# The low parts of `g` and of the expert weights, subtracted on VectorE instead of GpSimd

## The chip, the core and the metric

The kernel runs on one core of one Trainium2 chip. The metric is the device time of one execution in microseconds, as the median of several runs. The engines of a core are TensorE (PE: matrix products; PEld is its weight load), VectorE (DVE), ScalarE (ACT), GpSimd (POOL) and SyncE (SP, which here only issues DMAs). Each engine works through its own instructions in order and waits on semaphores for the others.

## What is computed

Three stages follow one another on 1792 tokens of 768 features:

```python
# 1. causal attention, 4 batches x 12 heads x 448 tokens x 64
scores = scale * np.matmul(q, k.transpose(0, 1, 3, 2))
scores = np.where(mask, -1000000000.0, scores)
x = softmax(scores) @ v                      # laid out as 1792 x 768
# 2. expansion with elu, 768 -> 2048 -> 768
h = x @ w_in
g = np.where(h > 0.0, h, alpha * (np.exp(np.minimum(h, 0.0)) - 1.0))
x = g @ w_out
# 3. routing to 8 experts of 224 tokens, in falling order of the logits
logits = x @ w_gate
order = np.argsort(-logits.flatten())        # greedy: one expert a token, at most 224 tokens an expert
for e in range(E):
    out[mask_e] = np.maximum(x[mask_e] @ w1[e], 0.0) @ w2[e]
```

## The kernel before, in words

**Products in two parts.** Where float32 accuracy is needed, an operand is split into a high part, which ScalarE copies into the format float32r, and a low part, the operand minus its high part. A product is then three products of TensorE: high by high, high by low, low by high. This gives the pairs of names `wh`, `wl` (weights), `xh`, `xl`, `gh`, `gl`. The change is about which engine subtracts the low parts.

**Stages.** Attention of the four batches runs interleaved with the first expansion (`gemm1`, L365), which writes `g` to DRAM as `gT_d`. Then comes the second expansion (`gemm2`, L592): 14 chunks of 128 tokens, for each 16 steps `m` of six products (L629). Every half chunk it loads a tile `gr` of 128x1024 (`load_g`), copies it to `gh` on ScalarE (L581) and subtracts `gl` (L582), which makes 28 of them. Beside it, interleaved into TensorE's order, runs the routing (`route`, L720): 7 phases, each with 7 search rounds. A round is a chain between VectorE and TensorE: `gg` (comparison, L757), products `lg` (L762), `fl` (L764), product `pv` (L767), `ju` (L770), next `gg`. A phase ends with `NB` (L798), products (L803, L806), `dd` (L809), a dozen small VectorE operations and the first `gg` of the next phase. Last come the 8 experts (`ffn`, L909). An expert's first half has 8 blocks of 6 pairs of products into a PSUM tile `h` (L928, L925; two buffers), each followed by `t` on ScalarE (L935), `t` on VectorE (L938), `ht` high on ScalarE (L941) and `ht` low on VectorE (L944). Its second half has 8 blocks of 12 products (L980), and TensorE's transposes of the next expert's tokens lie among them (L901). At its end the result `y` is copied (L956, L957) and scattered to `out` by an indirect DMA of GpSimd (L959); the next expert's tokens `xg` are gathered by two more (L889).

**Weights.** Each expert has 16 chunks of 128x768. `load_ck` loads one into one of 16 buffers `wr` through the sync engine's queue, 14 chunks ahead; `split_ck` copies it to `wh` on ScalarE (L504) and subtracts `wl` (L505), 7 chunks ahead of its use. Of 128 such chunks the even ones were subtracted on VectorE and the odd ones on GpSimd.

**Order.** The program is written by a small scheduler (`Sched`). Generators yield the estimated time of their products, and `after(d, fn)` puts a dependent operation behind them by `d` nanoseconds of that time. In the routing a negative yield says how much time of products of the second expansion lies before the next link of the chain:

```python
yield -1400 if n < 64 else -2200      # L759, between gg and lg
```

The operation then stands at that place in its engine's order, so that a subtraction placed between two links of the routing is executed between them.

Of the kernel before, what the change touches and what calls it, by code (L numbers as in the profile page):

```python
# [8 lines left out]
F32 = mybir.dt.float32  # L9
# [14 lines left out]
DM = H * D  # L24
KT = DM // 128
DF = 2048
MT = DF // 128
# [3 lines left out]
CAP = NTOK // E  # L31
# [3 lines left out]


class Sched:
    """Program order: products follow one another, and what depends on them is put behind
    them by about the time after which it can run."""

    def __init__(self):
        self.now, self.heap, self.n = 0.0, [], 0
# [1 line left out]
    def after(self, d, fn):  # L44
        self.n += 1
        tok = [False]
        heapq.heappush(self.heap, (self.now + d, self.n, fn, tok))
        return tok
# [28 lines left out]
def body(ctx, tc, q, k, v, w_in, w_out, w_gate, w1, w2, out, dbg=None):  # L77
    nc = tc.nc
    sch = Sched()
    after, need = sch.after, sch.need  # L80
    PE, V, A, G, SP = nc.tensor, nc.vector, nc.scalar, nc.gpsimd, nc.sync
# [5 lines left out]

    gT_d = dram.tile([128, MT, NTOK], F32, name="gT_d")

    # ---- constants  # L90
    ident = const.tile([128, 128], F32, name="ident")
    jp = const.tile([128, 128], F32, name="jp")
    mask = const.tile([128, S], F32, name="mask")
# [2 lines left out]
    wp = const.tile([128, MT, 32], F32, name="wp")  # L96
# [26 lines left out]
    for i in range(3):  # L123
        t = at.tile([128, NQ, 2, 64], F32, name=f"qz{i}", bufs=1)
        qz.append(t)

    # ---- loads
    KN, VN, WIN, STG = {}, {}, {}, {}

    def load_qk(n):  # L130
# [9 lines left out]
        SP.dma_start(VN[n][:, 0:3], v[b, j, 0:384].rearrange("(t p) h d -> p t h d", p=128))  # L140
        SP.dma_start(VN[n][:64, 3], v[b, j, 384:])

    # ---- float64 words to float32: bytes 3..6 hold the low exponent bits and the mantissa,
    # byte 7 the sign and the high exponent bits
    def load64_in(m):
        st = wf.tile([128, DM * 8], U8, name="st")
        STG[m] = st
        SP.dma_start(st[:, :DM * 8 - 3], w_in[m].bitcast(U8)[:, 3:])
# [38 lines left out]
        if nxt < MT:  # L187
            after(3100, lambda: load64_in(nxt))

    # ---- attention  # L190
    ST, XH, XL = {}, {}, {}

    def front(n):
# [91 lines left out]
            except StopIteration:  # L285
                st.remove(s)

    # ---- gate weights folded through w_out: wp = w_out @ w_gate, in stages of one chunk each
    def fold():
        ct, wt, wpt = {}, {}, {}  # L290

# [48 lines left out]

    WP = {}

    # ---- first expansion: gT = elu(w_in^T x)
    def logit4(pl, m, gs):
        for c in range(4):
            PE.matmul(pl[32 * c:32 * c + 32, :S], wp[:, m + c], gs[c],
# [71 lines left out]
    def logits(b, pl, tag):  # L418
        LT = wk.tile([128, S], F32, name="e")
        after(300, lambda: V.tensor_copy(LT, pl[:, :S]))  # L420

        # tokens on partitions
        def turn_logits():
            p = ps.tile([128, NQ, E], F32, name=tag, bufs=1)
            h, u = b * NQ, 0
            while u < NQ:
                n = 1 if (h + u) % 2 or u == NQ - 1 else 2
                o = 64 * ((h + u) % 2)
                PE.matmul(p[o:o + 64 * n, (h + u) // 2 - h // 2], LT[:, 64 * u:64 * (u + n)], sel, start=True, stop=True,
                          skip_group_check=True)  # L430
                u += n
            c0, c1 = (h + 1) // 2, (h + NQ) // 2
            V.tensor_copy(L[:, c0:c1], p[:, c0 - h // 2:c1 - h // 2])
            if h % 2:
                V.tensor_copy(L[64:, h // 2], p[64:, 0])
            else:
                V.tensor_copy(L[:64, c1], p[:64, c1 - h // 2])

        L_TOK.append(after(1500, turn_logits))
# [39 lines left out]
    def seq(*gs):  # L479
        for g in gs:  # L480
            yield from g

    sch.drive((seq(*[att_l(n) for n in range(-1, 6)]), 54000))
    for b in range(3):
        g = [(seq(*[att_l(n) for n in range(6 * b + 6, 6 * b + 12)]), 45000), (gemm1(b), 57600)]
# [11 lines left out]
    stAA.close()  # L497
    wA = ctx.enter_context(tc.tile_pool(name="wA", bufs=9, side="right"))

    # ---- weights of the later products: split into two parts that float32r carries  # L500
    def split(raw, pool, shape, e, gap=800):
        wh = pool.tile(shape, F32R, name="wh")
        wl = pool.tile(shape, F32R, name="wl")
        A.copy(wh, raw)  # L504
        return wh, wl, after(gap, lambda: e.tensor_sub(wl, raw, wh.bitcast(F32)))  # L505

    WO, WR = {}, {}
# [10 lines left out]
                yield -200  # L518
            WO[m] = split(WR.pop(m), wA, [128, DM], V)

    # logits of the first batch, from its part of gT
    def logits0():
        pl = ps.tile([128, 512], F32, name="pv", bufs=1)
        G0 = {}
# [15 lines left out]

    g0 = stA.enter_context(tc.tile_pool(name="g0", bufs=3))

    # ---- second expansion: x2 = g w_out
    # a row of zeros lies before the last chunk
    LAST = NTOK - 128
    x2_d = dram.tile([NTOK + 1, DM], F32, name="x2_d")
    stB, stW = ExitStack(), ExitStack()
    gb = stB.enter_context(tc.tile_pool(name="gb", bufs=3, side="right"))
    GR, GS = {}, {}

    # ---- weights of the experts: chunks of 128 rows of hidden features
    NCK = 2 * FT
    CK = {}

# [10 lines left out]

    def split_ck(i):
        if i < E * NCK:
            CK[i] = split(WR.pop(MT + i), wA, [128, DM], (V, G)[i % 2])
            load_ck(i + 14)

    def load_g(i):
# [5 lines left out]
    def split_g(i):  # L577
        t = GR.pop(i)
        gh = gb.tile([128, 8, 128], F32R, name="gh")
        gl = gb.tile([128, 8, 128], F32R, name="gl")  # L580
        A.copy(gh, t)  # L581
        GS[i] = gh, gl, after(1200, lambda: G.tensor_sub(gl, t, gh.bitcast(F32)))  # L582

    RT = []

# [59 lines left out]
        for _ in fg:  # L645
            yield 0

    # ---- the first expert's tokens: rows of the last chunk come from its product itself, by a
    # one-hot product, the others by a gather in which a row of zeros stands for those of the last chunk
    X2, PX, SLOT = {}, [], {}  # L650
    FIRST = {4: 1, 12: 1, 13: 1, 14: 1}

    def first_rows():
# [23 lines left out]
        for c in range(KT):  # L677
            PE.matmul(PX[c // 2][:, c % 2], o[:, c * 128:(c + 1) * 128], oh, start=False, stop=True,
                      skip_group_check=True)

    # ---- routing: the pairs in falling order of their logits, up to CAP tokens for an expert
    # keys of two parts: the upper 24 bits, then the lower 8 with the place of the token
    ROUNDS = (((18, 63), (12, 63), (6, 63), (0, 63)), ((12, 2 * NTOK // 32 - 1), (6, 63), (0, 63)))

    def consts_route(rt):
# [34 lines left out]
    def route():  # L720
# [55 lines left out]
        for ph in range(E - 1):  # L776
            V.tensor_tensor(lm, L, bc(pen, E), op=OP.add)
            V.tensor_reduce(m, lm, axis=AX.X, op=OP.max)
            # the bits of a float in an order of integers, in two halves
            V.tensor_scalar(mi, m.bitcast(I32), 31, -2 ** 31, op0=OP.arith_shift_right, op1=OP.bitwise_or)  # L780
            V.tensor_tensor(lm, lm, be(m, E), op=OP.is_equal)
            V.tensor_tensor(mi, mi, m.bitcast(I32), op=OP.bitwise_xor)
            V.tensor_tensor(lm, lm, bc(C["wt"], E), op=OP.mult)
            V.tensor_single_scalar(kh, mi, 8, op=OP.logical_shift_right)
            V.tensor_reduce(key, lm, axis=AX.X, op=OP.max)
            V.tensor_single_scalar(kl, mi, 0xFF, op=OP.bitwise_and)
            V.tensor_tensor(lm, lm, be(key, E), op=OP.is_equal)
            V.tensor_tensor(B, lm, be(un, E), op=OP.mult)
            V.scalar_tensor_tensor(m, kl, float(NTOK), C["rid"], op0=OP.mult, op1=OP.add)
            yield -1500 if ph else -9000  # L790
            th = yield from search(kh, 0.0, 0)
            V.scalar_tensor_tensor(key, kh, th, m, op0=OP.is_equal, op1=OP.mult)
            V.tensor_scalar(k2, kh, th, float(2 ** 20), op0=OP.is_gt, op1=OP.mult)
            V.tensor_add(key, key, k2)
            yield -500
            th = yield from search(key, 1.0, 1)
            V.tensor_scalar(k2, key, th, None, op0=OP.is_ge)
            V.tensor_tensor(NB_, B, be(k2, E), op=OP.mult)  # L798
            V.scalar_tensor_tensor(un, key, th, un, op0=OP.is_lt, op1=OP.mult)
            V.tensor_add(asg, asg, NB_)  # L800
            yield -400
            p = ps.tile([128, 512], F32, name="pv", bufs=1)
            PE.matmul(p[:, :NT * E], ones, NB_.rearrange("p c e -> p (c e)"), start=True, stop=True)  # L803
            p2 = ps.tile([128, 512], F32, name="lg", bufs=1)
            for c in range(NT):
                PE.matmul(p2[:E, :1], NB_[:, c], ones[:, :1], start=(c == 0), stop=(c == NT - 1))  # L806
            yield 400
            # a full expert takes no more part: its room is set beyond every count
            V.tensor_reduce(dd, p[:, :NT * E].rearrange("p (c e) -> p e c", e=E), axis=AX.X, op=OP.add)  # L809
            V.tensor_sub(rec[:E, 0:1], rec[:E, 0:1], p2[:E, :1])  # L810
            V.tensor_sub(rem, rem, dd)
            V.tensor_scalar(rec[:E, 1:2], rec[:E, 0:1], 0.5, 1.0e6, op0=OP.is_lt, op1=OP.mult)
            V.tensor_scalar(pen, rem, 0.5, -3.0e38, op0=OP.is_lt, op1=OP.mult)
            V.tensor_add(rec[:E, 0:1], rec[:E, 0:1], rec[:E, 1:2])
            yield -300
# [2 lines left out]
        V.tensor_add(asg, asg, B)  # L818
        V.memset(B, 0.0)
        yield -400  # L820
        # places within the experts, then the token of each place
        p = ps.tile([128, 512], F32, name="lg", bufs=1)
        PE.matmul(p[:, :NT * E], C["up"], asg.rearrange("p c e -> p (c e)"), start=True, stop=False,
                  skip_group_check=True)
# [53 lines left out]
    ex = ctx.enter_context(tc.tile_pool(name="ex", bufs=2))  # L878
    ix = IDX[0]

    # ---- experts
    XG = {}
    scat = []

# [24 lines left out]
    def ffn(e):  # L909
# [5 lines left out]
        for m in range(FT):  # L915
# [16 lines left out]
            t = ex.tile([128, 2, CAP], F32, name="t")  # L932
# [32 lines left out]
            after(300 + 400 * j, ev)  # L965

        W2 = {}
        # the last expert's halves follow one another, so that the first is written while the second is computed
        order = [(m, j) for j in range(2) for m in range(FT)] if e == E - 1 else \
            [(m, j) for m in range(FT) for j in range(2)]  # L970
        for m, j in order:
# [67 lines left out]
```

## Time and profile before

| | |
|---|---|
| median of 3 runs | 1116.58 us (1112.84 to 1119.04) |
| profiled execution: span from first to last instruction, the only time the page gives of it | 1113.1 us |
| PE busy | 1057.9 us, 95% |
| PEld busy | 881.7 us, 79% |
| DVE busy | 671.4 us, 60% |
| ACT busy | 438.9 us, 39% |
| POOL busy | 430.9 us, 39% |
| second expansion with routing | about 490 to 812 us of the span |
| experts | about 812 to 1106 us of the span |

Busy time is the time in which an engine has an instruction on record, and that holds time in which the instruction itself is held up. A wait is put down to what released it last. An `x2` behind a row of a timeline means two instructions in a row, merged. [...]

### The profile page before, as it was taken

The numbers are of one execution on the slowest core, as the hardware profiler recorded it, in microseconds if no ns is written. First come the engines' busy times: TensorE is split into PE (matmuls) and PEld (weight loads), VectorE is DVE, ScalarE is ACT, GpSimd is POOL, SyncE is SP. The second block draws the span as 40 slices with busy tenths as digits, with TensorE's granted clock in tenths as the row PEclk, the third lists the DMA queues.
The fourth block names the chain that finished last, engine by engine and source line by source line (L and its number), as shares of the span: only waits on it lengthen the run. The fifth ranks groups of instructions, "written<-read, shape, count | busy, mean of one in ns | idle before, by whom it ended". The sixth has DMA issues, their size and how long they took to land.

```text
span 1113.1 us, 17985 instructions
## 1 busy us (share of the span) xinstructions
PE 1057.9 (95%) x6615; PEld 881.7 (79%) x6615; DVE 671.4 (60%) x1596; ACT 438.9 (39%) x960; POOL 430.9 (39%) x467
## 2 busy tenths in 40 slices
PE   8999998999999999999999999989999999999997
PEld 4568676676777777878888888878988988898887
DVE  5889876777545445556545544553665466556652
ACT  5654444444445443432010001100255555455541
POOL 4465653444444440013222211322335455545542
PEclk9999999999999999999999999999999999999999
DMA  7646545666312106653233321220456676665710
GB/s 174 165 122 210 192 132 180 201 208 203 115 59 83 42 35 229 196 177 100 81 110 100 115 81 52 70 87 15 137 185 211 192 226 209 211 192 184 237 37 25
DMA packets 110858, 155.33 MB, mean 140 GB/s; under 512 B 29617, under 2 KB 82353, under 8 KB 110770
## 3 DMA queue, kind: packets, MB, share of 16 engines
q1 hardware_dynamic: 108210, 143.17, 40.8%
q0 software_dynamic: 2560, 11.01, 3.3%
q8 instruction: 52, 0.85, 0.3%
q14 instruction: 36, 0.29, 0.1%
HBM read 122.17 MB, written 31.98 MB: 138 GB/s over the span
## 4 chain that ended last, share of the span: by engine, by line
PE 77%; DVE 12%; issue 4%; ACT 4%; DMA 2%; SPq 0%; POOLq 0%; ACTq 0%; DVEq 0%; POOL 0%
PE h L629 11%; PE tp L629 9%; PE h L377 7%; PE sc L980 6%; PE h L379 6%; PE h L378 6%; PE h L928 5%; PE sc L200 5%; PE pv L262 4%; PE pv L980 3%; PE lg L980 3%; PE tp L248 3%; PE h L925 3%; PE lg L762 2%; DVE gg L757 2%
## 5 line engine op out<-in xcount | busy, mean ns | idle before, releaser
L582 POOL TENSOR_TENSOR gl<-gr,gh 128x1024 fp32r<-128x1024 f32 x28 | 72.2, 2595 | 305.1 <-ACT gh L581 195.6
L377 PE MATMUL h<-xh,wh 128*128 128x448 f32 x384 | 174.1, 453 | 0.0
L505 POOL TENSOR_TENSOR wl<-wr,wh 128x768 fp32r<-128x768 f32 x64 | 120.8, 1894 | 97.9 <-ACT wh L504 66.9
L928 PE MATMUL h<-xt,wh 128*128 128x448 f32 x384 | 130.1, 396 | 17.8 <-DVE t L938 17.8
L227 POOL TENSOR_SCALAR s<-s,sm 128x448 f32<-128x448 f32 (+6 forms) x168 | 98.4, 597 | 109.0 <-DVE sm L220 76.2
L379 PE MATMUL h<-xh,wl 128*128 128x448 f32 x384 | 140.5, 366 | 0.0
L378 PE MATMUL h<-xl,wh 128*128 128x448 f32 x384 | 140.2, 365 | 0.0
L212 ACT ACTIVATE s<-s,sm 128x448 f32<-128x448 f32 (+6 forms) x168 | 85.1, 507 | 136.5 <-DVE sm L208 135.1
L362 POOL TENSOR_TENSOR wl<-wr,wh 128x768 fp32r<-128x768 f32 x48 | 92.0, 1918 | 103.7 <-ACT wh L361 97.6
L504 ACT CAST wh<-wr 128x768 fp32r<-128x768 f32 x144 | 118.2, 829 | 31.3 <-PE lg L980 19.1
L639 ACT COPY x<-h 128x384 f32<-128x384 f32 x14 | 6.7, 480 | 261.5 <-PE h L629 261.5
L505 DVE TENSOR_TENSOR wl<-wr,wh 128x768 fp32r<-128x768 f32 x80 | 90.8, 1139 | 30.1 <-ACT wh L504 29.6
L377 PEld LDWEIGHTS h<-xh,wh 128*128 128x128 f32 x384 | 72.4, 189 | 37.3 <-issue 28.8
L208 DVE CUSTOM_DVE_ANT_0 s<-sc,mask 128x448 f32<-128x448 f32 (+6 forms) x150 | 62.1, 420 | 61.8 <-PE sc L200 56.2
L925 PE MATMUL h<-xt,wl 128*128 128x224 f32 x384 | 96.3, 278 | 0.0
L200 PE MATMUL sc<-kT,qz 128*128 128x192 f32 (+6 forms) x300 | 92.1, 395 | 1.9 <-DMA kT<-in_k_dram 1.0
L928 PEld LDWEIGHTS h<-xt,wh 128*128 128x128 f32 x384 | 73.6, 202 | 24.8 <-DVE t L938 20.1
L629 PE MATMUL h<-wh,gh 128*128 128x384 f32 x224 | 87.3, 390 | 0.0
L378 PEld LDWEIGHTS h<-xl,wh 128*128 128x128 f32 x384 | 72.8, 190 | 8.7 <-issue 3.0
L925 PEld LDWEIGHTS h<-xt,wl 128*128 128x128 f32 x384 | 78.0, 203 | 2.0
L379 PEld LDWEIGHTS h<-xh,wl 128*128 128x128 f32 x384 | 72.2, 188 | 6.1
L629 PE MATMUL h<-wl,gh 128*128 128x384 f32 x224 | 76.1, 340 | 0.3 <-DVE wl L505 0.3
(206 smaller groups left out, 2292.7 us busy)
## 6 DMA issues: line engine op xcount, KB each, us to landing
wr<-in_moe_w_dram SPq DMA_DIRECT2D x128, 384.0 KB, 3.6
gT_d<-g SPq DMA_DIRECT2D x64, 224.0 KB, 1.9
gr<-gT_d SPq DMA_DIRECT2D x28, 512.0 KB, 4.2
st<-in_moe_w_in_dram SPq DMA_DIRECT2D x16, 767.6 KB, 4.5
st<-in_moe_w_out_dram SPq DMA_DIRECT2D x16, 767.6 KB, 5.0
wo_d<-wo SPq DMA_DIRECT2D x16, 384.0 KB, 3.0
wr<-wo_d SPq DMA_DIRECT2D x16, 384.0 KB, 3.8
qz<-in_q_dram SPq DMA_DIRECT2D x48, 112.0 KB, 3.6
```

Of the source, the lines that this page charges most:

```text
L200: PE.matmul(p[:, :w], qT[:, i].rearrange("p a c -> p (a c)"), kT[:, :w], start=True, stop=True)
L227: G.tensor_scalar(s[:, :w], s[:, :w], sm[:, 2, i:i + 1], 1.0, op0=OP.mult, op1=OP.mult)
L362: t = after(800, lambda: (V if b == 3 else G).tensor_sub(wl, WIN[m], wh.bitcast(F32)))
L377: PE.matmul(p[:, :S], wh[:, c], xh, start=(c == 0), stop=False)
L378: PE.matmul(p[:, :S], wh[:, c], xl, start=False, stop=False)
L379: PE.matmul(p[:, :S], wl[:, c], xh, start=False, stop=(c == KT - 1))
L504: A.copy(wh, raw)
L505: return wh, wl, after(gap, lambda: e.tensor_sub(wl, raw, wh.bitcast(F32)))
L629: PE.matmul(p[n][:, :384], st[:, mm], wsel[:, 384 * n:384 * n + 384], start=(m == 0 and first), stop=(m == MT - 1 and st is gl))
L925: PE.matmul(p[:, :CAP], wl[:, c], xt[:, c, :CAP], start=False, stop=stop, skip_group_check=True)
L928: PE.matmul(p[:, :2 * CAP], wh[:, c], xt[:, c], start=(c == 0), stop=(c == KT - 1), skip_group_check=True)
L980: PE.matmul(acc[j][n][:HC, :384], ht[:, m, s, j * HC:(j + 1) * HC], wsel[:, 384 * n:384 * n + 384], start=(m == 0 and first), stop=(m == F ...
```

## The change

In `split_ck` all weight chunks of the experts now give their subtraction to VectorE (`V`) instead of to VectorE and GpSimd (`G`) in turn, and in `split_g` the subtraction of `gl` is VectorE's. Nothing else is changed but comments, which are left out here.

```diff
     def split_ck(i):
         if i < E * NCK:
-            CK[i] = split(WR.pop(MT + i), wA, [128, DM], (V, G)[i % 2])
+            CK[i] = split(WR.pop(MT + i), wA, [128, DM], V)
             load_ck(i + 14)
...
     def split_g(i):
         t = GR.pop(i)
         gh = gb.tile([128, 8, 128], F32R, name="gh")
         gl = gb.tile([128, 8, 128], F32R, name="gl")
         A.copy(gh, t)
-        GS[i] = gh, gl, after(1200, lambda: G.tensor_sub(gl, t, gh.bitcast(F32)))
+        GS[i] = gh, gl, after(1200, lambda: V.tensor_sub(gl, t, gh.bitcast(F32)))
```

TensorE's 6016 and ScalarE's 731 rows of the program are the same and stand in the same order. On VectorE 28 rows of `gl` and 64 of `wl` are added. Three places show it.

VectorE at the end of an expert's first half, before (the last blocks of the first expert, `t`, `wl` and `ht`, and the first `wl` of its second half):

```order
L938 TENSOR_TENSOR t_8556<-h_8538,t_8556 128x224
L505 TENSOR_TENSOR wl_8558<-wr_8198,wh_8557 128x768
L944 SCALAR_TENSOR_TENSOR ht_8392<-t_8556,ht_8392 128x224
L938 TENSOR_TENSOR t_8580<-h_8562,t_8580 128x224
L944 SCALAR_TENSOR_TENSOR ht_8392<-t_8580,ht_8392 128x224
L505 TENSOR_TENSOR wl_8608<-wr_8254,wh_8607 128x768
```

The same place now:

```order
L938 TENSOR_TENSOR t_8556<-h_8538,t_8556 128x224
L505 TENSOR_TENSOR wl_8558<-wr_8198,wh_8557 128x768
L944 SCALAR_TENSOR_TENSOR ht_8392<-t_8556,ht_8392 128x224
L938 TENSOR_TENSOR t_8580<-h_8562,t_8580 128x224
L505 TENSOR_TENSOR wl_8586<-wr_8233,wh_8585 128x768
L944 SCALAR_TENSOR_TENSOR ht_8392<-t_8580,ht_8392 128x224
```

A `wl` stands between `t` and `ht` in every block, where it stood in every second one.

GpSimd between two experts, before (`xg` the gathers, `out_dram` the scatters, `spacer` a memset of one element):

```order
L889 DMA xg<-x_d,ig 112x768 x2
L958 MEMSET spacer 1x1
L959 DMA out_dram<-y,ix 1792x768
L505 TENSOR_TENSOR wl<-wr,wh 128x768 x8
L958 MEMSET spacer 1x1
L959 DMA out_dram<-y,ix 1792x768
```

The same place now:

```order
L889 DMA xg<-x_d,ig 112x768 x2
L958 MEMSET spacer 1x1
L959 DMA out_dram<-y,ix 1792x768
L958 MEMSET spacer 1x1
L959 DMA out_dram<-y,ix 1792x768
```

The eight subtractions are gone, and DMA issues and memsets of one element are what remains in GpSimd's order.

VectorE in the routing, the difference at two places, a search round and the end of a phase:

```order
 L754 MEMSET base_5347 128x1
 L757 SCALAR_TENSOR_TENSOR gg_5348<-key_5352,base_5347,tab12_5310 128x14x111
+L582 TENSOR_TENSOR gl_6048<-gr_5817,gh_6047 128x1024
 L764 TENSOR_SCALAR fl_5350<-lg_6056,rec_5336 8x111
 L770 TENSOR_SCALAR ju_5351,base_5347<-pv_6079,base_5347 128x111
...
 L799 SCALAR_TENSOR_TENSOR un_5330<-key_5352,base_5347,un_5330 128x14
 L800 TENSOR_TENSOR asg_5332<-asg_5332,NB_5346 128x112
+L582 TENSOR_TENSOR gl_6169<-gr_5929,gh_6168 128x1024
 L809 TENSOR_REDUCE dd_5349<-pv_6181 128x8
 L810 TENSOR_TENSOR rec_5336<-rec_5336,lg_6183 8x1
```

Of the 28 `gl`, 20 now stand between a `gg` and its `fl`, as in the first piece. The other eight: two among the last operations of the first expansion, one ahead of the first phase's search, one ahead of a phase's second search, one ahead of `dd` (second piece), one ahead of a phase's first `gg`, one ahead of the operations that make `NB`, and one behind the last phase.

## Rows read from the trace of the kernel before

**Rows 1.** Page, busy us, share of the span, instructions.
```profile
PE 1057.9 (95%) x6615; PEld 881.7 (79%) x6615; DVE 671.4 (60%) x1596; ACT 438.9 (39%) x960; POOL 430.9 (39%) x467
```

**Rows 2.** Waits of TensorE from 485 us on: us in total, times, longest.
```profile
PE h L928 <- DVE t L938: 17.8, 8, 2.3
PE lg L762 <- DVE gg L757: 10.9, 8, 3.8
PE pv L803 <- DVE NB L798: 2.4, 1, 2.4
```

**Rows 3.** Timeline of VectorE in the seventh expert: start us, us, instruction, idle before.
```profile
1039.64 4.49 DVE L944 SCALAR_TENSOR_TENSOR ht<-t,ht 128x224 fp32r<-128x224 f32 x1 [0.46 <-ACT ht L941]
1044.05 0.38 DVE L938 TENSOR_TENSOR t<-h,t 128x224 f32<-128x224 f32 x1
1044.35 0.94 DVE L505 TENSOR_TENSOR wl<-wr,wh 128x768 fp32r<-128x768 f32 x1
1045.22 0.38 DVE L944 SCALAR_TENSOR_TENSOR ht<-t,ht 128x224 fp32r<-128x224 f32 x1
1045.85 0.39 DVE L938 TENSOR_TENSOR t<-h,t 128x224 f32<-128x224 f32 x1 [0.25 <-ACT t L935]
```

**Rows 4.** Timeline of GpSimd, same stretch.
```profile
1039.28 0.96 POOL L959 DMA_INDIRECT out_dram<-y,ix  x1 [0.22 <-issue]
1040.26 3.61 POOL L505 TENSOR_TENSOR wl<-wr,wh 128x768 fp32r<-128x768 f32 x2
```

**Rows 5.** Timeline of TensorE, same stretch.
```profile
1044.48 0.47 PE L928 MATMUL h<-xt,wh 128*128 128x448 f32 x1 [2.33 <-DVE t L938]
```

**Rows 6.** Timeline of VectorE in the second expansion.
```profile
525.24 1.14 DVE L757 SCALAR_TENSOR_TENSOR gg<-kh,base,tab 128x882 bf16<-128x882 int32 x1
527.70 0.27 DVE L764 TENSOR_SCALAR fl<-lg,rec 8x63 bf16<-8x63 f32 x1 [1.31 <-PE lg L762]
...
550.28 1.14 DVE L757 SCALAR_TENSOR_TENSOR gg<-kh,base,tab 128x882 bf16<-128x882 int32 x1
...
742.61 2.19 DVE L811 TENSOR_TENSOR rem<-rem,dd 128x8 f32<-128x8 f32 x1
```

**Rows 7.** Timeline of GpSimd at the last of these.
```profile
742.38 4.74 POOL L582 TENSOR_TENSOR gl<-gr,gh 128x1024 fp32r<-128x1024 f32 x2 [17.34 <-ACT gh L581]
```

**Rows 8.** Busy times by expert: stretch, length, PE, PEld, DVE, ACT, POOL, PEclk, DMA, GB/s.
```profile
849.30:886.60 37.30, 34.99 (x205) 33.46 (x205) 21.26 (x29) 19.88 (x38) 19.23 (x14) 0.95 0.66 207
886.60:922.40 35.80, 33.46 (x206) 32.12 (x205) 21.97 (x29) 19.66 (x38) 19.32 (x14) 1.00 0.68 215
```

**Rows 9.** Busy times of two stretches of the second expansion, columns as in rows 8.
```profile
550.00:600.00 50.00, 47.56 (x357) 41.71 (x356) 24.15 (x67) 5.51 (x8) 9.40 (x4) 0.97 0.29 90
...
750.00:812.00 62.00, 60.50 (x442) 55.70 (x442) 30.33 (x69) 11.42 (x17) 16.09 (x8) 0.97 0.23 75
```

**Rows 10.** Instructions by tile and line: count, ns min/median/max, first and last start.
```profile
L505 DVE TENSOR_TENSOR wl<-wr,wh x80: 940/948/6394, 439.1 to 1088.6; 128x768 fp32r<-128x768 f32 x80
...
L269 DVE TENSOR_TENSOR xl<-pv,xh x24: 602/624/625, 19.2 to 422.2; 128x448 fp32r<-128x448 f32 x24
...
L582 POOL TENSOR_TENSOR gl<-gr,gh x28: 2337/2398/3442, 490.7 to 791.1; 128x1024 fp32r<-128x1024 f32 x28
```

**Rows 11.** The last expert's first half on TensorE, columns as in rows 10.
```profile
L928 PE MATMUL h<-xt,wh x48: 362/375/473, 1071.7 to 1089.0; 128*128 128x448 f32 x48
```

**Rows 12.** Timeline of TensorE at the second phase's first `gg`.
```profile
551.76 0.57 PE L762 MATMUL lg<-gg,B 128*8 128x63 bf16 x14
```

**Rows 13.** Timeline of GpSimd in the first expert.
```profile
815.56 0.93 POOL L889 DMA_INDIRECT xg<-x_d,ig  x1 [11.57 <-DMA x_d<-x]
```

**Rows 14.** Timeline of VectorE in the first expert.
```profile
815.58 0.96 DVE L505 TENSOR_TENSOR wl<-wr,wh 128x768 fp32r<-128x768 f32 x1
```

## The prediction

> **What bounds the kernel now.** I read the page's busy shares first, then the list of who waited for whom on TensorE, then the timelines of single engines at the stalls, and last the busy times cut at the eight experts. TensorE is busy 95% of the span, VectorE 60% [rows 1]. So work that moves from GpSimd to VectorE has no price by itself. It counts only where TensorE waits for VectorE, or would begin to.
>
> After the first expansion TensorE has three waits worth counting, and all are for VectorE [rows 2]: 17.8 us in 8 waits for `t` (L938) in the experts, 10.9 us in 8 waits for `gg` (L757) and 2.4 us in one wait for `NB` (L798), both in the routing that runs beside the second expansion. The reader is to see that the other lines of that list, left out here, stay under 0.6 us each.
>
> What holds VectorE? Each expert shows the same picture near its start. `ht` (L944), an operation of 0.38 us, is on record with 4.49 us: the fourth row against the first of [rows 3]. GpSimd runs a DMA issue and then two weight subtractions (L505) back to back from 1040.26 for 3.61 us [rows 4], so to 1043.87, and the next `t` starts at 1044.05. TensorE, which has two PSUM buffers `h` and needs one of them back, goes on at 1044.48 after 2.33 us of waiting [rows 5]. So an elementwise operation on GpSimd and a VectorE operation with two SBUF inputs exclude one another, and GpSimd's next one goes ahead of the waiting VectorE. Routing shows it as well: `rem` (L811), on 8 columns, is on record with 2.19 us from 742.61, while GpSimd runs two `gl` subtractions (L582) from 742.38 for 4.74 us [rows 6, 7].
>
> A stall is dearer than its wait. The expert from 886.6 has its wait too, but keeps a granted clock of 1.00 and takes 35.80 us; its neighbour reads 0.95 and takes 37.30 [rows 8]. [...] One such drop costs 37.3 - 35.8 = 1.5 us. In the second expansion two stretches read 0.97 [rows 9]; the two longest waits there, 2.4 and 3.8 us, end in them.
>
> **What the change removes.** In the experts 64 subtractions leave GpSimd; its queue keeps DMA issues and one-element memsets. Nothing elementwise is left to hold `ht` or a VectorE `wl`. I let all eight waits go, 17.8 us, and six clock drops, 6 x 1.5 = 9.0. Experts: 26.8 us. In the second expansion the 28 `gl` go, and with them the cause of the `gg` and `NB` waits: 10.9 + 2.4 = 13.3 us, and two drops, 3.0. Together 16.3 us. Next in line behind these waits are TensorE's own products.
>
> **What it adds.** 64 `wl` of 128x768 at VectorE's median of 948 ns [rows 10] are 60.7 us. A `gl` of 128x1024 has never run on VectorE. The nearest rows are 768 columns at 948 ns and 448 columns at 624 ns [rows 10], or 1.01 ns a column: 948 + 256 x 1.01 = 1207 ns, an estimate. Bounds: not under 948, for it has more columns; not over GpSimd's 2398 [rows 10]. I take 1.21 us, next to the row of the same operation on the same engine. 28 of them are 33.8 us.
>
> Experts: eight more `wl` an expert are 7.6 us. VectorE is busy 21.3 us of an expert [rows 8], held time included, so it comes to 28.9 at worst, of the 35.8 - 2.3 = 33.5 us that an expert takes without its wait. What matters is the first half, where a block of twelve products recurs. In the last expert the 48 pairs fill 1071.7 to 1089.0 [rows 11]; less a wait of 2.2 (17.8 / 8), over 8 blocks, a block is 1.9 us. VectorE's share of it is `t` 0.38, `wl` 0.94, `ht` 0.38: 1.70 us. In a block that has this full set already, the next `t` follows 1.80 us behind the last, 1044.05 to 1045.85 [rows 3]. That is under 1.9, so each block's `wl` hides beside the products. The cover is thin, 0.1 us a block; once it is gone every block costs what it lacks.
>
> Second expansion: 20 of the 28 `gl` come between a `gg` and its `fl`. VectorE waits there for TensorE's products: in the undisturbed round `gg` ends at 525.24 + 1.14 = 526.38 and `fl` starts at 527.70, with 1.31 us idle ahead of it [rows 6]. 1.21 us fit, at no cost to TensorE; if they did not, `pv` would come later. Two lie in the chain from `dd` to the next phase's first `gg`. That `gg` ends at 550.28 + 1.14 = 551.42 and TensorE starts on it at 551.76 [rows 6, 12], a cover of 0.34 us: 2 x (1.21 - 0.34) = 1.7 us. One lies ahead of `NB`; no row shows its cover, so I take it as fully exposed: 1.2. The five others I cost at nothing: four lie outside the phases, where TensorE's list has no wait of note, and one ahead of the wide search, for whose products the schedule leaves 2200 in place of 1400 (L759). If that cover is missing too, each is 1.2. Sum: 2.9 us.
>
> ScalarE and TensorE issue the same rows in the same order. The sync engine's queue refills a weight buffer once `wl` has read it; on VectorE that comes earlier. GpSimd's gathers and scatters no longer queue behind subtractions. None of it is waited for by TensorE, and I cost it at nothing.
>
> **The sum.** 26.8 + 16.3 - 2.9 = 40.2 us off a span of 1113.1 gives 1072.9. That span lies 3.5 us under the median of the runs, 1116.58; against the median the forecast is 1076.4 us.
>
> **A row against a rule.** DMA issues stay on GpSimd. In the seventh expert `ht` starts at 1039.64, inside an issue that runs from 1039.28 to 1040.24, and is held through its end [rows 3, 4]. In the first expert an issue of 0.93 us and a `wl` of 0.96 us lie on top of each other, and neither is stretched [rows 13, 14]. I go by the second pair, since in the first the subtractions behind the issue explain the hold, and price the issues at nothing.
> [...]
>
> **Rivals.**
> One: ScalarE and VectorE pace the expert blocks. For it: 0.1 us of cover a block. Against it: the block with the full set that the trace has, measured behind a stall, when both engines were catching up. If the cycle became 2.1 us, 64 x 0.2 = 12.8 us come back: 1089 us. [...]
> Two: GpSimd's DMA issues still hold VectorE. Four fall into the first 5 us of an expert, 0.96 us each [rows 4]; VectorE would lose up to 3.8 us there. With waits and clock drops kept at half, 26.8 / 2 = 13.4 us come back: 1090 us. For it: the first pair of rows above; against it: the second.
> Three, slower than before: `gl` does not fit between `gg` and `fl`, and each of the 26 in the routing delays TensorE by all its 1.21 us with a clock drop of 1.5 behind it: 26 x 2.7 = 70 us in place of 2.9, so 1116.6 - 43.1 + 70 = 1144. It decides from a delay of 43.1 / 26 = 1.7 us for each. Against it: 1.31 us of idle before `fl`.
> That the change does not do what it says is excluded by the order of the instructions.
>
> **How the numbers follow.** Forecast 0.74, rival one 0.13, rival two 0.08, rival three 0.03; 0.02 for a gain that is lost to within 0.5%, about what a measurement of this kernel can tell from no change. Faster is then 0.95, the same 0.02, slower 0.03. The forecast's own range is 1067 to 1083. Below: no new wait (2.9), drops of 1.9 us in place of 1.5, which a mean clock of 0.95 over 37.3 us would give if all of it were lost (8 x 0.4 = 3.2), and a median some 3 us nearer to the span. Above: a clock drop behind each of the three charged waits (4.5) and one or two of the uncharged `gl` exposed. To leave out no more than 2 in 10, the range reaches up to rivals one and two: 1067 to 1090.
>
> **What would show it.** Right: no `ht` over 1 us and every VectorE `wl` of 768 columns near 0.95; TensorE's wait for `t` gone from the list; experts at 33.4 to 33.7 us with a clock of 1.00; `gl` at 1.2 us; `gg` of 882 columns at 1.14; new TensorE waits of about 1 us for `gg` or `NB` at two or three phase ends. Wrong: waits for `t` that recur in many blocks (rival one) or stay at the experts' starts under a DMA issue (rival two), or waits for `pv` and `gg` in every round (rival three).

## The result, and the profile after

The changed kernel takes 1077.03 us as the median of 4 runs (1073.82 to 1077.82), beside 1115.88 us for the kernel before on the same chip: a ratio of 0.965 (95% interval 0.962 to 0.968). In a second comparison it took 1076.69 us, ratio 0.9647 (0.9619 to 0.9674). The forecast was 1076.4 us. The profiled execution is the fastest of the four (1073.82 us); by the medians the gain is 38.9 us.

The head of the page after, with TensorE's and VectorE's busy times:

```profile
span 1072.0 us, 17898 instructions
...
PE 1044.8 (97%) x6615; PEld 871.5 (81%) x6615; DVE 679.4 (63%) x1688; ACT 440.1 (41%) x960; POOL 247.3 (23%) x375
```

GpSimd's share falls from 39% to 23%, yet VectorE's rises only from 60% to 63% [rows 1]: what it took on is nearly what it no longer spends held. TensorE runs the same 6615 products, so the span splits into its busy time and the rest, in which it waits. The busy time moved with the mean of TensorE's granted clock (PEclk, a share of full speed), 0.986 before and 0.998 after: 1057.9 x 0.986 = 1043.1 and 1044.8 x 0.998 = 1042.7, nearly the same. Before, busy time and rest were 1057.9 + 55.2, after 1044.8 + 27.2. Of the 41.1 us of span (1113.1 - 1072.0), waiting gave 28.0 and the clock 13.1.

TensorE's list of waits after the first expansion, in the changed kernel (who waited, for whom: us in all, times, longest):

```profile
PE sc L671 <- DMA gr<-x_d,i: 3.1, 2, 2.3
PE lg L762 <- DVE gg L757: 0.8, 1, 0.8
PE pv L803 <- DVE NB L798: 0.7, 1, 0.7
...
```

Against [rows 2] the wait for `t` is gone, `gg` has fallen from 10.9 us to 0.8 and `NB` from 2.4 to 0.7. At the top stands a wait that the list of before does not have: the first expert's products `sc` (L671) wait 3.1 us for gathered rows.

VectorE's instructions, one row for each line and output (count: shortest/median/longest in ns, first and last start in us):

```profile
L505 DVE TENSOR_TENSOR wl<-wr,wh x144: 943/949/984, 438.6 to 1049.2; 128x768 fp32r<-128x768 f32 x144
L582 DVE TENSOR_TENSOR gl<-gr,gh x28: 1215/1219/1226, 490.1 to 774.6; 128x1024 fp32r<-128x1024 f32 x28
L944 DVE SCALAR_TENSOR_TENSOR ht<-t,ht x64: 376/383/390, 805.1 to 1050.0; 128x224 fp32r<-128x224 f32 x64
L757 DVE SCALAR_TENSOR_TENSOR gg<-kh,base,tab x28: 1139/1141/1144, 511.0 to 745.4; 128x882 bf16<-128x882 int32 x28
```

Nothing is held any more: `wl` went up to 6.39 us before and `ht` to 4.49 [rows 3, 10], now all 144 and all 64 lie within 5% of their median.

Two experts cut at their own length of 33.0 us (columns: PE, PEld, DVE, ACT and POOL busy with their counts, granted clock, DMA share, GB/s):

```profile
834.00:867.00 33.00, 33.00 (x205) 31.92 (x204) 22.67 (x37) 19.88 (x38) 5.06 (x6) 1.00 0.73 231
867.00:900.00 33.00, 33.00 (x205) 31.93 (x204) 22.51 (x38) 19.88 (x38) 5.18 (x6) 1.00 0.73 231
```

TensorE has no idle time in an expert and the full clock, where it had 35.8 us at best and 37.3 in most [rows 8].

Where the gain fell is read from the first start of the experts' product L925. First the kernel before, then the changed one:

```profile
L925 PE MATMUL h<-xt,wl x384: 262/266/419, 812.6 to 1088.9; 128*128 128x224 f32 x192
```

```profile
L925 PE MATMUL h<-xt,wl x384: 262/266/277, 801.1 to 1047.9; 128*128 128x224 f32 x192
```

From there to the end it was 1113.1 - 812.6 = 300.5 us and is 1072.0 - 801.1 = 270.9: **29.6 us in the experts**. The second expansion (first product L629 at 492.6 before, 492.0 after) went from 320.0 to 309.1 us: **10.9 us**.

The new wait begins at VectorE. First its rows, then GpSimd's, then TensorE's, all of the changed kernel (start, duration, instruction, idle time ahead of it and its releaser):

```profile
778.53 5.29 DVE L505 TENSOR_TENSOR wl<-wr,wh 128x768 fp32r<-128x768 f32 x6
798.05 0.56 DVE L640 COPY x<-tp 128x384 f32<-128x384 f32 x1 [14.24 <-PE tp L629]
```

```profile
779.14 5.69 POOL L663 DMA_INDIRECT gr<-x_d,i  x1 [286.26 <-DVE oh L658]
785.13 0.94 POOL L663 DMA_INDIRECT gr<-x_d,i  x1 [0.30 <-issue]
```

```profile
788.26 0.47 PE L671 MATMUL sc<-ident,gr 112*128 112x112 f32 x2 [2.32 <-DMA gr<-x_d,i]
789.53 0.92 PE L671 MATMUL sc<-ident,gr 112*128 112x112 f32 x6 [0.79 <-DMA gr<-x_d,i]
790.22 0.55 PE L629 MATMUL h<-wh,gh 128*128 128x384 f32 x1
```

GpSimd begins the first gather's issue 0.6 us into a row of six `wl`, which ends at 783.82; the issue ends at 784.83, about its usual 0.95 us later. So the gathers land late, TensorE waits, and behind that its clock falls: it reads 0.59 from 790 to 792 us, 0.56 to 794 and 1.00 again to 796, and the next L629 takes 0.52 to 0.55 us in place of 0.34. Right after the six `wl` VectorE has 14.24 us without work.

### The profile page after: what moved, and what is told of

The parts are those of the page before. It is cut to its first block, busy times and chain, and to the rows that moved or that the text cites. A ratio compares the mean times of both kernels' runs of the same rounds, so it can differ in the third digit from the quotient of the medians.

```text
span 1072.0 us, 17898 instructions
## 1 busy us (share of the span) xinstructions
PE 1044.8 (97%) x6615; PEld 871.5 (81%) x6615; DVE 679.4 (63%) x1688; ACT 440.1 (41%) x960; POOL 247.3 (23%) x375
## 4 chain that ended last, share of the span: by engine, by line
PE 85%; DVE 7%; ACT 2%; issue 2%; DMA 1%; POOL 1%; SPq 0%; POOLq 0%; DVEq 0%; ACTq 0%
PE h L629 12%; PE tp L629 10%; PE h L928 8%; PE h L377 7%; PE sc L980 6%; PE h L379 6%; PE h L378 6%; PE sc L200 5%; PE pv L262 4%; PE h L925 4%; PE pv L980 3%; PE lg L980 3%; PE tp L248 3%; PE lg L762 2%; ACT s L212 1%
## 5 line engine op out<-in xcount | busy, mean ns | idle before, releaser
L505 DVE TENSOR_TENSOR wl<-wr,wh 128x768 fp32r<-128x768 f32 x144 | 135.5, 952 | 17.5 <-ACT wh L504 17.2
L928 PE MATMUL h<-xt,wh 128*128 128x448 f32 x384 | 119.2, 373 | 0.0
L362 POOL TENSOR_TENSOR wl<-wr,wh 128x768 fp32r<-128x768 f32 x48 | 92.3, 1924 | 103.7 <-ACT wh L361 97.6
L377 PEld LDWEIGHTS h<-xh,wh 128*128 128x128 f32 x384 | 72.4, 189 | 37.3 <-issue 28.8
L925 PE MATMUL h<-xt,wl 128*128 128x224 f32 x384 | 92.1, 267 | 0.0
L629 PE MATMUL h<-wh,gh 128*128 128x384 f32 x224 | 86.9, 388 | 0.0
L629 PE MATMUL tp<-wh,gl 128*128 128x384 f32 x224 | 75.6, 337 | 0.0
L629 PE MATMUL tp<-wh,gh 128*128 128x384 f32 x224 | 75.4, 337 | 0.0
L629 PE MATMUL h<-wl,gh 128*128 128x384 f32 x224 | 75.3, 336 | 0.0
L629 PE MATMUL tp<-wl,gh 128*128 128x384 f32 x224 | 75.2, 336 | 0.0
L629 PE MATMUL h<-wh,gl 128*128 128x384 f32 x224 | 75.2, 336 | 0.0
```

What stands on the lines that cost most here:

```text
L377: PE.matmul(p[:, :S], wh[:, c], xh, start=(c == 0), stop=False)
L629: PE.matmul(p[n][:, :384], st[:, mm], wsel[:, 384 * n:384 * n + 384], start=(m == 0 and first), stop=(m == MT - 1 and st is gl))
L925: PE.matmul(p[:, :CAP], wl[:, c], xt[:, c, :CAP], start=False, stop=stop, skip_group_check=True)
L928: PE.matmul(p[:, :2 * CAP], wh[:, c], xt[:, c], start=(c == 0), stop=(c == KT - 1), skip_group_check=True)
```

## The experiments

**Each half alone.** Two kernels, each shown as its difference to the changed kernel. The first undoes the move of `gl`, so that `wl` alone is moved; the second undoes that of `wl`.

```diff
-        GS[i] = gh, gl, after(1200, lambda: V.tensor_sub(gl, t, gh.bitcast(F32)))
+        GS[i] = gh, gl, after(1200, lambda: G.tensor_sub(gl, t, gh.bitcast(F32)))
```

```diff
-            CK[i] = split(WR.pop(MT + i), wA, [128, DM], V)
+            CK[i] = split(WR.pop(MT + i), wA, [128, DM], (V, G)[i % 2])
```

> Only the experts' wl moves to VectorE; gl stays on GpSimd. Theory (an elementwise operation of GpSimd excludes VectorE operations with two SBUF inputs): the experts shorten by all of 29.7 us, from 293.9 to 264.2; the waits of the second expansion for gg and NB (13.3 us) and their clock drops stay; TensorE waits for the first expert's gather (3.1 us and a drop) as with the full change, for VectorE's burst of six wl is the same: 1116 - 29.7 + 4.6, so about 1091 us. Rival (what counts is that VectorE finishes a weight earlier than GpSimd, not the exclusion): gl is waited for by nobody, so all of the gain is there: 1077 us.

> Only gl moves to VectorE; the experts' odd wl stay on GpSimd. Theory: the waits for gg and NB shrink from 13.3 to about 1.5 us and two clock drops go, 15 us in all: about 1101 us, with the eight waits for t (17.8 us) untouched and no long wait for the first expert's gather, since GpSimd's own three wl come behind it. Rival (adding 34 us of gl to VectorE costs the routing what it saves): 1116 us.

Measured: `wl` alone 1091.35 us (ratio 0.9783, 0.9751 to 0.9815), `gl` alone 1100.43 us (0.9854, 0.9828 to 0.9881), with 1117.37 us for the kernel before on that chip. They gain 26.0 and 16.9 us; the sum, 42.9, is the 40.0 of both together (1116.73 - 1076.69, in the second comparison), to within the scatter of the runs. TensorE's waits, first with `wl` alone, then with `gl` alone:

```profile
PE lg L762 <- DVE gg L757: 10.9, 8, 3.8
PE sc L671 <- DMA gr<-x_d,i: 3.7, 2, 3.4
PE pv L803 <- DVE NB L798: 2.4, 1, 2.4
```

```profile
PE h L928 <- DVE t L938: 17.3, 8, 2.3
PE lg L762 <- DVE gg L757: 0.8, 1, 0.8
PE pv L803 <- DVE NB L798: 0.7, 1, 0.7
```

Each half removes its own waits and leaves the other's as they were. The gather wait comes with `wl` alone and not with `gl` alone. With `gl` alone the experts' first L925 starts here:

```profile
L925 PE MATMUL h<-xt,wl x384: 262/266/419, 796.6 to 1073.9; 128*128 128x224 f32 x192
```

With its L629 from 492.8, that second expansion takes 303.8 us, 16.2 less than before; the full change gives only 10.9. The 5.3 us between them are the price of the new gather wait: 3.1 us of waiting, and 2.2 us by which TensorE's busy time in the stage is longer (303.1 against 300.9).

**What of GpSimd's work holds VectorE.** The changed kernel gets GpSimd work back at 61 of the 64 odd weight chunks of the experts, whose result nobody uses: subtractions that read one tile twice; memsets of the same size, which write only (behind a copy of one element); and subtractions of two different tiles.

```diff
             CK[i] = split(WR.pop(MT + i), wA, [128, DM], V)
+            if i % 2 and JUNK:
+                z = CK[i][0].bitcast(F32)
+                after(800, lambda: G.tensor_sub(JUNK[0], z, z))
```

The lines that make the scratch tiles `JUNK` are left out here and below. The kernel with memsets has `G.tensor_copy(spacer, z[:1, :1])` and twice `G.memset(JUNK[0], 0.0)` in the place of the subtraction, the one with two tiles `G.tensor_sub(JUNK[0], z, JUNK[1])`.

> The full change, and GpSimd again runs a subtraction of 128x768 at each place where it had one in the experts, on a finished wh, into a scratch tile that nobody reads. VectorE still makes every wl. Theory (exclusion): the waits for t come back, 17 us and several clock drops: about 1104 us. Rival (an earlier wl is what counts): nobody waits for the scratch tile, 1077 us.

> As the run before, but GpSimd's extra work writes only: one element is copied from the finished wh, then two memsets of 128x768 fill the scratch tile. [...]

> The changed kernel with GpSimd subtractions of 128x768 at each odd chunk of the experts, as in the kernel with reading ghosts, but with two different input tiles in place of one read twice. That kernel took 1093.7 us with ghosts of 1.49 us, where 1104 was expected. Theory (the subtractions that the change removed cost what they did because of their length, 1.86 us, and the ghosts read twice were merely shorter): they read about 1.86 us, VectorE is held 0.37 us longer by each, and the time comes to 1100 to 1106 us, with TensorE's waits for `t` near 17 us. Rival (length aside, their place in the queue sets it, since the removed ones ran back to back behind gathers): longer ghosts, but waits for `t` no more than 12 us and 1094 to 1097 us.

Measured: reading 1093.7 us (ratio 0.9791, 0.9758 to 0.9824); writing 1074.07 us (0.9615, 0.9583 to 0.9648); two tiles 1109.82 us (0.9944, 0.9925 to 0.9964). GpSimd's rows in the three:

```profile
L572 POOL TENSOR_TENSOR junk<-wh x61: 1466/1486/2227, 809.2 to 1070.3; 128x768 f32<-128x768 f32 x61
```

```profile
L576 POOL MEMSET junk<- x122: 727/739/749, 807.4 to 1050.1; 128x768 f32 x122
```

```profile
L572 POOL TENSOR_TENSOR junk<-wh,src x61: 1836/1858/2624, 808.2 to 1085.3; 128x768 f32<-128x768 f32 x61
```

With the memsets, 90 us of GpSimd work in all, TensorE's list of waits is that of the changed kernel, and `ht` stays here:

```profile
L955 DVE SCALAR_TENSOR_TENSOR ht<-t,ht x64: 377/385/388, 805.5 to 1050.7; 128x224 fp32r<-128x224 f32 x64
```

So it is not GpSimd being busy that holds VectorE: its subtractions, which read SBUF, do (VectorE's `wl` is on record with up to 2.65 us beside those of one tile and 2.94 beside those of two), and its memsets, which only write, do not (1.01 us at most). Nor is it that a weight is subtracted earlier on VectorE: VectorE makes every `wl` in all three kernels, nobody waits for the scratch tile, and yet the subtractions cost time. A GpSimd operation that reads one tile once was not run. With subtractions of two tiles TensorE's waits for VectorE in the experts are:

```profile
PE h L935 <- DVE t L945: 16.6, 13, 2.2
PE tp L908 <- DVE xt L911: 5.0, 5, 1.7
```

Sixty-one subtractions of 1.86 us cost 33 us, more than the 26.0 that the move of `wl` alone gained. The reading ones missed their expectation (1104); one tile read twice takes 1.49 us, which I had not allowed for. Those of two tiles overshot theirs (1106 at most) by 3.8 us: the waits for `t` are the 17 us expected, and 5.0 us of waits for `xt` come on top, probably because VectorE now carries every `wl` itself. How the two engines take turns differs from what I read in [rows 3, 4]. First VectorE, then GpSimd, with the reading subtractions:

```profile
881.79 2.16 DVE L505 TENSOR_TENSOR wl<-wr,wh 128x768 fp32r<-128x768 f32 x1
883.87 1.65 DVE L949 SCALAR_TENSOR_TENSOR ht<-t,ht 128x224 fp32r<-128x224 f32 x1
885.44 0.38 DVE L943 TENSOR_TENSOR t<-h,t 128x224 f32<-128x224 f32 x1
```

```profile
881.64 5.20 POOL L572 TENSOR_TENSOR junk<-wh 128x768 f32<-128x768 f32 x3
```

Three subtractions of 1.49 us would take 4.5 us and take 5.2. VectorE's `wl` and `ht` are each 1.2 to 1.3 us longer than undisturbed, less than one subtraction, so each was passed by one at most: the two engines alternate here. Before, a waiting `ht` was passed by two GpSimd operations in a row [rows 3, 4]. What decides whose turn it is stays open.

**The new gather wait.** Four memsets on VectorE, of a tile no longer needed, stand behind the gathers in the code, so the six `wl` begin only when both issues have gone out. A variant has `V.tensor_copy(SLOT["gg"], SLOT["lo"])` there, a copy that reads one bf16 tile of 1568 columns. One more line, left out here, hands the tile `gg` over. The changed kernel ran again beside the first.

```diff
             xg.append(t)
+        for _ in range(4):
+            V.memset(SLOT["gg"], 0.0)
         yield -7000
```

> The changed kernel itself again, as the base for the next two on the same chip. Expected: 1077 us as before, with the wait of 3.1 us of TensorE for the first expert's gathers (`sc` L671) and no wait for `t`. If the wait were chance, the first gather issue would read about 0.95 us here in place of 5.7.

> The changed kernel with four VectorE memsets of an unused tile of 1568 columns in two bytes put behind the issue of the first expert's two gathers, where VectorE has some 14 us without work later on. They read no SBUF, and put off the burst of six `wl` that lies on the issue. Theory (VectorE's two-input operations hold the issue, which reads its list of rows from SBUF): the two issues read about 0.95 and 1.3 us in place of 5.7 and 0.9, TensorE's wait of 3.1 us for the gathers goes and with it the clock drop behind it, 1.5 us: about 4.6 us less than the changed kernel, 1072 us. Rival (GpSimd's issue is slow there for another reason, or VectorE holds it whatever VectorE does): the issue stays at 5 us or more and the time at 1077 us, or above it by the wl put off.

> As the kernel with four memsets behind the first expert's gathers, but with four VectorE copies of a 1568-column bf16 tile in their place, so that VectorE reads one SBUF operand beside the issues. Theory (only VectorE operations with two SBUF inputs hold the issue, or the sheer reading of one does not): the issues stay near 1 us and the time at 1070.6 us. Rival (any reading of SBUF by VectorE at full rate holds it): the first issue is stretched until the copies end, by some 2 to 4 us, and TensorE's wait for the gathers comes back in part: 1073 to 1077 us.

Measured: the changed kernel 1076.69 us (1074.29 to 1077.77, 5 runs), with the memsets **1070.59 us** (1068.64 to 1070.92, 5 runs): ratio to the kernel before 0.9591 (0.9565 to 0.9617), and 6.1 us under the changed kernel. No version but the one with copies is as fast. VectorE's and GpSimd's rows with the memsets:

```profile
783.30 0.71 DVE L667 MEMSET gg<- 128x784 uint32 x1 [0.23 <-DVE gg L667]
783.93 5.23 DVE L505 TENSOR_TENSOR wl<-wr,wh 128x768 fp32r<-128x768 f32 x6
```

```profile
780.88 1.13 POOL L663 DMA_INDIRECT gr<-x_d,i  x1 [286.25 <-DVE oh L658]
782.32 0.94 POOL L663 DMA_INDIRECT gr<-x_d,i  x1 [0.30 <-ACT wh L504]
```

The six `wl` are as long as ever and start later, the issues take 1.13 and 0.94 us, and the wait for `gr` has left TensorE's list. The second expansion takes 303.8 us again (first L629 at 493.8, first product of the experts at 797.6), as with `gl` alone; in the repeat of the changed kernel it takes 310.8. The gain is over the 4.6 us expected. In that repeat the first issue took 5.70 us, so the long issue was not chance; the wait was 3.4 us, and the stretch behind it had this clock (columns as in the windows above):

```profile
790.00:800.00 10.00, 9.72 (x46) 9.50 (x47) 0.00 (x0) 0.00 (x0) 0.00 (x0) 0.66 0.00 0
```

A clock of 0.66 over 10 us is 3.4 us of time lost, so wait and drop make 6.8, where I had 1.5 for the drop; in the first profile of the changed kernel the same stretch reads 0.83, or 1.7 us.

With copies in place of the memsets the time is the same, 1070.3 us in two runs (ratio 0.9586, 0.9536 to 0.9636):

```profile
781.20 1.32 POOL L663 DMA_INDIRECT gr<-x_d,i  x1 [286.23 <-DVE gg L667]
782.82 0.99 POOL L663 DMA_INDIRECT gr<-x_d,i  x1 [0.30 <-ACT wh L504]
```

Copies with one source lie under the whole first issue and lengthen it by some 0.4 us at most, where the row of `wl` cost 4.7. The second issue starts 0.1 us ahead of the six `wl`, which begin at 782.92 here, and runs beside them at its usual 0.99 us. So it was the row of `wl` on the issue that made the gather late. Which of the two engines goes first does not follow from which starts first, though. With `gl` alone the same issue comes as far into a row of two `wl` and is through when the row is (VectorE, then GpSimd):

```profile
779.29 2.01 DVE L505 TENSOR_TENSOR wl<-wr,wh 128x768 fp32r<-128x768 f32 x2
779.91 1.34 POOL L663 DMA_INDIRECT gr<-x_d,i  x1 [286.25 <-DMA wr<-in_moe_w_dram]
```

And in the experts a scatter's issue that starts 0.15 us ahead of a single `wl` is held by it (the rows under rival two below).

**How thick the cover of an expert block is.** The changed kernel gets one more VectorE operation in each of the 64 blocks.

```diff
                 A.activation(ht[:, m, 0], t[:, 1], AF.Relu)
+                V.memset(JUNK[0][:, :384], 0.0)
```

> The changed kernel with one more VectorE operation in each block of the experts' first half: a memset of 384 columns in four bytes, by an estimate from the other rows of VectorE 0.3 to 0.4 us, 64 in all, so some 22 us more of VectorE's time. It tests the cover that the prediction gave a block. By the prediction's 0.1 us of cover each block lacks 0.2 to 0.3 us: 64 x 0.25 = 16 us, 1093 us, with waits for `t` in many blocks. By the idle of 0.3 to 0.4 us that the changed kernel's timeline shows ahead of each `t`: all of it hides, 1077 to 1080 us.

Measured: 1077.2 us (1073.34 to 1078.32; ratio 0.9643, 0.9609 to 0.9677), against 1076.69 for the changed kernel on the same chip. The memsets and one block's VectorE instructions:

```profile
L944 DVE MEMSET junk<- x64: 378/378/378, 809.1 to 1054.4; 128x384 f32 x64
```

```profile
879.76 0.39 DVE L940 TENSOR_TENSOR t<-h,t 128x224 f32<-128x224 f32 x1
880.07 0.95 DVE L505 TENSOR_TENSOR wl<-wr,wh 128x768 fp32r<-128x768 f32 x1
881.04 0.38 DVE L944 MEMSET junk<- 128x384 f32 x1
881.34 0.33 DVE L947 SCALAR_TENSOR_TENSOR ht<-t,ht 128x224 fp32r<-128x224 f32 x1
881.65 0.39 DVE L940 TENSOR_TENSOR t<-h,t 128x224 f32<-128x224 f32 x1
```

24.2 us of VectorE work cost 0.5 us, which the runs can't tell from nothing. The four durations add up to 2.05 us, yet the next `t` starts 1.89 us after the last: consecutive records overlap, so the starts give an engine's pace and the durations overstate it. Here the cover is used up: VectorE has no idle time left in the block, and TensorE still does not wait.

## Why the prediction was right, point by point

**The experts' waits: right, the clock undersized.** All eight waits for `t` went, as "I let all eight waits go, 17.8 us" has it. The stage gave 29.6 us, not 26.8: what is left for the six clock drops is 29.6 - 17.8 = 11.8, or 2.0 us each in place of 1.5. No row ahead of the prediction shows that there were six; the trace of before does: the clock reads 0.95 in six experts and 1.00 in the third and the last, and behind the seventh's wait 0.54 from 1045 to 1047 us and 0.60 to 1049, with L928 at 0.60 us in place of 0.37 to 0.38. An expert takes 33.0 us, just under the 33.4 to 33.7 I looked for. The better price was the one that I kept for the range, 1.9 from a mean clock of 0.95 over 37.3 us; the 1.5 came from one pair of neighbours, and the faster of them, with 33.46 us of TensorE's time [rows 8], was not free of loss: an expert now has 33.00.

**The second expansion: right in its mechanism.** With `gl` alone the stage gives 16.2 us. The forecast was "Together 16.3 us", less 2.9 for new waits: 13.4. The new waits, for `gg` and `NB`, came to 0.8 + 0.7 = 1.5, and TensorE's busy time in the stage fell by 4.1 us (305.0 to 300.9) where I had 3.0 for two clock drops. A `gl` takes 1.219 us on VectorE (estimate 1.21), `gg` of 882 columns 1.14, and no other `gl` is waited for.

**What failed: "None of it is waited for by TensorE, and I cost it at nothing."** I asked only whether GpSimd's issues hold VectorE. The price lay the other way: VectorE's row of six `wl`, half of which were GpSimd's before, holds the first expert's gather for 4.7 us, and TensorE paid 5.3 (7.0 in the repeat). It was mended by moving the row behind the issue, for 6.1 us. A sign of it lay in the trace of the kernel before: I put the four issues at an expert's start at 0.96 us each, but in six of seven the second gather took 1.43 to 1.49 there, beside a `wl` that had begun just ahead of it (VectorE, then GpSimd):

```profile
1037.21 0.95 DVE L505 TENSOR_TENSOR wl<-wr,wh 128x768 fp32r<-128x768 f32 x1
1037.48 1.49 POOL L889 DMA_INDIRECT xg<-x_d,ig  x1 [0.30 <-issue]
```

The sentence holds in seven experts, where TensorE waits for no gather; the first one's gathers come at the very end of routing, and it waited 3.1 us for them. The terms that were off the other way made up for it: 29.6 us in place of 26.8 in the experts, 16.2 in place of 13.4 in the second expansion. So the total came out close to what was forecast, 41.1 us of span against 40.2. The two main terms were right for their reasons; that the sum came so close is luck.

**Rival one fell**, and the step that fed it was too dark: the cover of a block is not 0.1 us: a memset of 0.38 us fits into it. The 1.80 us that I set against the block's 1.9 hold 0.25 us in which VectorE waits for ScalarE [rows 3]; its own part, from 1044.05 to the end of `ht` at 1045.60, is 1.55. The sum of 1.70 us was too high as well, since it adds up durations that overlap.

**Rival two fell.** In an expert of the changed kernel, issues and VectorE's operations lie together like this, GpSimd first:

```profile
867.85 1.93 POOL L959 DMA_INDIRECT out_dram<-y,ix  x1 [27.17 <-ACT wh L504]
870.08 0.96 POOL L889 DMA_INDIRECT xg<-x_d,ig  x1 [0.30 <-issue]
```

```profile
868.00 0.95 DVE L505 TENSOR_TENSOR wl<-wr,wh 128x768 fp32r<-128x768 f32 x1
870.10 0.97 DVE L505 TENSOR_TENSOR wl<-wr,wh 128x768 fp32r<-128x768 f32 x1
```

No `wl` and no `ht` of the changed kernel is stretched by an issue, as [rows 13, 14] had it. The hold of `ht` in [rows 3, 4] needed the subtractions behind the issue; that it began 0.62 us ahead of the first of them is not explained. The issue, however, is stretched: this scatter takes 1.93 us and ends 0.83 us behind the `wl`. The seven scatters at this place take 1.82 to 1.94 us; before, where VectorE had no `wl` there, they took 0.96 to 0.98. Nothing waits for them.

**Rival three fell**: TensorE waits for `gg` and `NB` once each (0.8 and 0.7 us), not 26 times.

**"GpSimd's next one goes ahead of the waiting VectorE"** described the kernel before and is no rule: the reading subtractions alternated with VectorE's operations.

**Who held whom.** Reading subtractions on GpSimd held VectorE and memsets did not. The first expert's gather was held the other way round, by VectorE: a row of two-source subtractions did it, 5.69 us in place of 0.94, and one-source bf16 copies hardly, 1.32.

## What to carry to other kernels

Subtractions on GpSimd, which read SBUF, were paid by VectorE here, in its operations with two SBUF inputs (before, `wl` took up to 6.39 us and `ht` up to 4.5, while `t`, which has one of its inputs in PSUM, stayed at 0.39): 92 subtractions moved from GpSimd raised VectorE's busy time by 8 us only, and shortened the span by 41. Before moving work, look in both directions: a row of two-source VectorE operations can hold a DMA issue on GpSimd's queue (here six of them, 5.69 us in place of 0.94), and if the transfer is due soon, put the issue ahead of the row. Price a stall by its wait plus its clock drop (here some 2 us), and an engine's load by the distance of its starts (here 1.89 us a block, where the durations add up to 2.05).

## What the runs showed of the hardware

GpSimd subtracts 128x768 in 1.49 us when both inputs are one tile, and in 1.86 us when they are two. GpSimd memsets of 128x768 (0.74 us) left VectorE's subtractions at a median of 0.95 us. A DMA issue on GpSimd's queue that started 0.6 us into a row of six VectorE subtractions took 5.69 us in place of 0.94, but one that came as far into a row of two, with `gl` alone, took 1.34. An issue that started ahead of a VectorE subtraction ran beside it at 0.93 to 0.99 us in some places (0.02 us ahead for the gather at 870.08, 0.10 with the copies), and took 1.82 to 1.94 us in others (the scatters, 0.02 to 0.16 us ahead). What decides it stays open. The clock drop behind one and the same wait of 3.1 to 3.4 us cost 1.7 us in one profile (0.83 over 10 us) and 3.4 in another (0.66).
